# Moving eight modulation chunks, spreading transposes, and ordering a softmax behind a copy in an adaLN attention and FFN block

## The chip, the cores and the metric

The kernel runs on one core of a Trainium2 chip. The metric is the device time of one execution, in microseconds (us), lower being better. Times are medians of several executions, and all executions used here are fast. "Span" is the length of the one execution that was profiled; it was 1.7 to 2.2 us shorter than the time of the same execution in the runs here.

Names in the profile: PE is TensorE (matrix multiplications and transposes), PEld its weight loads, DVE is VectorE, ACT is ScalarE, POOL is GpSimd, and SP issues loads. PSUM is the memory that the matmuls here write to, and an eviction is a copy out of it. Each trace also keeps a record of the clock that TensorE was granted, the clock record below; a slow spell is a stretch of it at half clock. In the kernel before, one lasts from 63.33 to 66.74 us: matmuls with 512 columns start 0.43 us apart in it, and 0.215 us apart at full clock (from 55.63 us, for instance).

## The reference

```python
# x: (1, 2048, 1024), c: (1, 1024), w_mod: (1024, 6*1024), F = 3584
mod = (silu(c) @ w_mod).reshape(c.shape[0], 6, 1, -1)
sa, ca, ga, sb, cb, gb = mod[:, 0], ..., mod[:, 5]
h = layernorm(x) * (1 + ca) + sa
x = x + ga * A(h, wqkv, wo)          # 32 heads of 32; each position looks at 8 positions, 2 apart
h = layernorm(x) * (1 + cb) + sb
x = x + gb * B(h, w_gate, w_up, w_down)   # (sigmoid(h @ w_gate) * (h @ w_up)) @ w_down
```

## The kernel before

The 2048 rows are worked in four chunks of 512: chunks 0 and 1 are the first halves of the even and of the odd rows, chunks 2 and 3 the second halves. A chunk is projected to q, k and v on TensorE, which are stored to DRAM and loaded back in the layout that attention needs. Attention itself is VectorE's work: four units per chunk, each with products, sums, one Exp on ScalarE, and products again. Then TensorE transposes the attention result `Ot` into `oT`, multiplies it by `wo`, VectorE adds it to `X`, a second layernorm gives `Z`, TensorE transposes that into `h2T`, and the FFN follows.

The vector `mod` is made in twelve chunks of 512 columns. Each needs 1 MB of `w_mod`:

```python
    def mod_chunk(cc, col=None, add=0.0, dst=None, mul=1.0):
        wm = ring.tile([P, KT, 512], BF, name="wm", tag="w")
        nc.sync.dma_start(wm[:], w_mod[:, cc * 512:(cc + 1) * 512].rearrange(...))
        ps = ptile("aux", "ps_mod")
        for kt in range(KT):                       # 8 matmuls
            nc.tensor.matmul(ps[32 * j:32 * j + 32, :], sc_pad[:, kt, :], wm[:, kt, :], ...)
        part = small.tile([P, 512], BF, name="part")
        nc.scalar.copy(part[:], ps[:])             # ScalarE
        cv = ptile("aux", "cv")
        if dst is None:
            ...                                    # 4 small matmuls, then VectorE writes 4 columns
            nc.vector.tensor_scalar_add(modc[:, col:col + 4], cv[:, 0:4], add)
        else:
            ...
```

The order of the first half of the kernel is this. All eight later mod chunks stand between the layernorm of chunk 1 and the projection of chunk 0:

```python
    load_x(0)
    mod_cols(0, 0)                  # mod chunks 0 to 3
    ...                             # loads of wqkv and of X of chunk 1
    prep_chunk(0, tag="mm", split=True)   # layernorm, 32 transposes, evictions into hT
    for ci in range(NCH - 1):
        if ci + 2 < NCH:
            load_x(ci + 2)
        prep_chunk(ci + 1)
        if ci == 0:
            mod_bcast(4, ga_bc, 1.0)      # mod chunks 4, 5
            mod_cols(6, 2 * KT)           # 6 to 9
            mod_bcast(10, gbh_bc, 0.5)    # 10, 11
        ...                               # for the last: load wo and scale it by ga
        qkv_chunk(ci, range(NQ))
        if ci == 0:
            attention_chunk(0)            # at low priority: fills gaps on VectorE
    qkv_chunk(NCH - 1, range(NSPLIT))
    ...
    wo_chunk(0)
    qkv_chunk(NCH - 1, range(NSPLIT, NQ))
    ...
    for ci in range(NCH):
        if ci + 1 < NCH:
            attention_chunk(ci + 1)
            wo_chunk(ci + 1)
        ffn_a(ci)
        ffn_b(ci, last=(ci == NCH - 1))
```

A scheduler turns this into one fixed instruction order per engine before the kernel runs. In the trace of the kernel before, ScalarE keeps to its order even where it costs time: it stands idle for 6.23 us before an Exp while copies stand behind it whose transposes had ended at 192.35 us (below).

## Time and profile before

| | before |
|---|---|
| time, median (lowest to highest) | 900.81 us (899.01 to 902.83), 16 executions |
| span of the profile | 897.1 us |
| TensorE busy | 845.6 us |
| VectorE busy | 532.7 us, most of it before 504.6 us, where the last attention result is written |

From the profile's page of the kernel before: the busy time of each engine with its share of the span, and below it the rows in which each digit is one fortieth of the span (22.4 us) and gives the busy share in tenths.

```profile
PE 845.6 (94%) x4145; PEld 389.3 (43%) x4228; DVE 532.7 (59%) x652; ACT 194.8 (22%) x318; POOL 42.4 (5%) x71
...
PE   3979989969999999989999999999999999999997
...
DVE  4458999999799999999989612144121023121122
```

TensorE is nearly always busy, so its gaps are few and can be looked at one by one. VectorE is as full as TensorE in the first half of the kernel and has much room in the second.

The timeline of TensorE in the kernel before, at its three longest gaps between 30 and 245 us. The columns are start, duration, engine, line, operation, output and inputs, shapes, count; the bracket gives the idle time just before and what ended it.

```profile
63.62 1.04 PE L135 MATMUL ps_mod<-wm,sc_pad 128*32 128x512 bf16 x8 [4.37 <-DMA wm<-in_w_mod_dram]
...
129.28 0.61 PE L177 MATMUL tp<-ident,Xt 128*128 128x128 bf16 x8 [2.98 <-ACT hT L188]
...
199.67 1.01 PE L177 MATMUL tp<-ident,Ot 128*128 128x128 bf16 x8 [6.47 <-ACT oT L179]
```

The first is a wait for a mod chunk's weights. In the second, 32 transposes stand together, and each group of eight needs a PSUM buffer that ScalarE must have emptied. The third is a copy of transposes on ScalarE that came late. ScalarE's own timeline tells why:

```profile
191.49 0.59 ACT L237 CAST stg<-ps_qkv 128x512 bf16<-128x512 f32 x1 [1.14 <-PE ps_qkv L234]
198.31 0.42 ACT L282 ACTIVATE Et<-Lt 128x256 f32<-128x256 f32 x1 [6.23 <-DVE Lt L280]
198.63 1.91 ACT L179 COPY oT<-tp 128x1024 bf16<-128x1024 bf16 x2
```

ScalarE stood idle for 6.23 us for the Exp, whose input VectorE had not finished, and the copies that TensorE needed stood behind that Exp. The first two of those copies were ready to run: the sixteen transposes that they copy had ended at 192.35 us.

VectorE has its own waits. Its timeline in the kernel before, at the three longest after 50 us:

```profile
56.60 4.49 DVE L264 TENSOR_TENSOR prod<-qt,kh 128x4096 bf16<-128x4096 bf16 x2 [4.48 <-DMA qt<-qs]
...
70.03 0.16 DVE L143 TENSOR_SCALAR modc<-cv 128x4 f32<-128x4 f32 x1 [6.61 <-PE cv L142]
...
237.99 0.60 DVE L284 TENSOR_REDUCE sm<-Et 128x32 f32<-128x256 f32 x1 [4.75 <-ACT Et L282]
```

These are waits for the first q tile (loaded back from DRAM among the `w_mod` loads: its store took 9.0 us to land and its load 6.4), for a mod chunk on TensorE, and for an Exp.

### The profile page before, as it was taken

How to read it: one execution, taken by the hardware profiler on the slowest of the kernel's cores; microseconds unless marked ns; L12 is line 12 of the kernel's file. 1: busy time of each engine (PE TensorE's matmuls, PEld its weight loads, DVE VectorE, ACT ScalarE, POOL GpSimd, SP SyncE). 2: the span in 40 equal slices, each digit the busy share in tenths (PEclk: the TensorE clock that was granted, in tenths of full speed). 3: DMA queues.
4: the chain of work that ended last, by engine and by line, in shares of the span. 5: the costliest groups of instructions: out<-in, count | busy, mean ns of one | idle time of the engine just before them, and what ended most of it. 6: DMA issues, size and time to landing. Idle time of an engine off the chain costs nothing.

```text
span 897.1 us, 10091 instructions
## 1 busy us (share of the span) xinstructions
PE 845.6 (94%) x4145; PEld 389.3 (43%) x4228; DVE 532.7 (59%) x652; ACT 194.8 (22%) x318; POOL 42.4 (5%) x71
## 2 busy tenths in 40 slices
PE   3979989969999999989999999999999999999997
PEld 1434444434444444434444444444444444444443
DVE  4458999999799999999989612144121023121122
ACT  2436353331521232002132110023111001111100
POOL 0020100010100000001000000000000000000000
PEclk9999999989999999989999999999999999999999
DMA  9999847461345465757524455441544555453541
GB/s 304 359 335 373 287 167 266 151 236 40 114 164 171 126 213 184 269 172 254 181 94 140 142 164 164 157 172 47 188 129 141 165 175 173 156 179 108 175 149 47
DMA packets 125310, 162.20 MB, mean 181 GB/s; under 512 B 4160, under 2 KB 108608, under 8 KB 125264
## 3 DMA queue, kind: packets, MB, share of 16 engines
q1 hardware_dynamic: 117472, 126.95, 43.3%
q0 software_dynamic: 7792, 34.61, 11.1%
q8 instruction: 33, 0.54, 0.2%
q14 instruction: 13, 0.11, 0.0%
HBM read 144.71 MB, written 16.83 MB: 180 GB/s over the span
## 4 chain that ended last, share of the span: by engine, by line
PE 42%; DVE 32%; issue 18%; DMA 5%; ACT 2%; POOL 1%; SPq 0%; POOLq 0%; DVEq 0%; ACTq 0%
PE y L400 11%; PE ups L354 10%; PE gps L350 10%; DVE prod L264 6%; DVE prod L270 5%; DVE pv L292 5%; PE ps_qkv L234 4%; PE ps_wo L328 3%; DVE pv L297 3%; DVE hh L359 2%; DVE ln_st L161 2%; PE yl L389 2%; DMA wm<-in_w_mod_dram 2%; DVE pv L298 1%; PE tp L177 1%
## 5 line engine op out<-in xcount | busy, mean ns | idle before, releaser
L350 PE MATMUL gps<-h2T,wg 128*128 128x512 bf16 x874 | 212.8, 379 | 1.5 <-ACT stg L237 0.2
L354 PE MATMUL ups<-h2T,wu 128*128 128x512 bf16 x876 | 213.3, 379 | 0.9
L400 PE MATMUL y<-wd,hh 128*128 128x512 bf16 x770 | 172.1, 383 | 4.5 <-DVE ytmp L379 3.7
L359 DVE SCALAR_TENSOR_TENSOR hh<-th,ups 128x512 bf16<-128x512 f32 x112 | 76.5, 683 | 166.1 <-PE ups L354 157.4
L234 PE MATMUL ps_qkv<-wq,hT 128*128 128x512 bf16 x749 | 171.2, 382 | 1.3 <-issue 0.5
L357 ACT ACTIVATE th<-gps 128x512 f32<-128x512 f32 x112 | 66.9, 597 | 370.6 <-PE gps L350 303.7
L350 PEld LDWEIGHTS <-wg 128*128 128x128 bf16 x896 | 87.3, 98 | 103.1 <-issue 0.3
L354 PEld LDWEIGHTS <-wu 128*128 128x128 bf16 x896 | 87.3, 98 | 102.8
L400 PEld LDWEIGHTS <-hh 128*128 128x128 bf16 x784 | 77.3, 99 | 98.6 <-issue 7.6
L234 PEld LDWEIGHTS <-hT 128*128 128x128 bf16 x768 | 74.2, 98 | 89.2 <-issue 5.0
L379 DVE TENSOR_TENSOR ytmp<-y,gbh_bc 128x512 f32<-128x512 f32 x28 | 18.0, 682 | 107.9 <-PE y L400 107.9
L264 DVE TENSOR_TENSOR prod<-qt,kh 128x4096 bf16<-128x4096 bf16 x32 | 72.3, 2284 | 4.8 <-DMA qt<-qs 4.5
L270 DVE TENSOR_TENSOR prod<-prod 128x4096 bf16<-128x4096 bf16 (+1 forms) x64 | 73.7, 1152 | 1.3
L292 DVE TENSOR_TENSOR pv<-vh,A 128x4096 bf16<-128x4096 bf16 x32 | 72.3, 2286 | 0.4
L328 PE MATMUL ps_wo<-wo_sb,oT 128*128 128x512 bf16 x251 | 61.5, 382 | 1.5 <-DVE X L330 1.2
L239 ACT CAST stg<-ps_qkv 128x512 bf16<-128x512 f32 x64 | 37.0, 591 | 62.9 <-PE ps_qkv L234 61.8
L328 PEld LDWEIGHTS <-oT 128*128 128x128 bf16 x256 | 24.5, 99 | 32.9 <-issue 5.5
L297 DVE TENSOR_TENSOR pv<-pv 128x4096 bf16<-128x4096 bf16 x16 | 36.5, 2281 | 0.2
L179 ACT COPY oT<-tp 128x1024 bf16<-128x1024 bf16 x16 | 16.1, 1011 | 73.1 <-PE tp L177 73.0
L330 DVE TENSOR_TENSOR X<-ps_wo,X 128x512 bf16<-128x512 f32 x32 | 21.8, 684 | 11.0 <-PE ps_wo L328 6.4
L161 DVE BATCH_NORM_STATS2 ln_st<-Xt 128x6 f32<-128x512 bf16 x32 | 19.9, 665 | 12.3 <-DMA Xt<-in_A_x_dram 12.3
L188 ACT ACTIVATE h2T<-tp,modc 128x512 bf16<-128x512 bf16 x32 | 22.8, 778 | 10.8 <-PE tp L177 10.8
(64 smaller groups left out, 372.2 us busy)
## 6 DMA issues: line engine op xcount, KB each, us to landing
wg<-in_B_w_gate_dram SPq DMA_DIRECT2D x28, 1024.0 KB, 5.3
wu<-in_B_w_up_dram SPq DMA_DIRECT2D x28, 1024.0 KB, 7.2
wd<-in_B_w_down_dram SPq DMA_DIRECT2D x32, 896.0 KB, 5.2
wm<-in_w_mod_dram SPq DMA_DIRECT2D x12, 1024.0 KB, 8.1
kh<-ks POOLq DMA_DIRECT2D x16, 704.0 KB, 6.0
vh<-vs POOLq DMA_DIRECT2D x16, 704.0 KB, 4.7
wq<-in_A_wqkv_dram SPq DMA_DIRECT2D x6, 1024.0 KB, 12.5
Xt<-in_A_x_dram SPq DMA_DIRECT2D x4, 1024.0 KB, 9.4
```

What stands on the lines that cost most here:

```text
L161: nc.vector.bn_stats(st[:, b, hf, :], Xt[:, b, hf * 512:(hf + 1) * 512])
L234: nc.tensor.matmul(ps[:], hT[:, kt, b * P:(b + 1) * P], wt[:, kt, :], start=(kt == 0), stop=(kt == KT - 1))
L264: nc.vector.tensor_tensor(prod[:, 4 * i:4 * i + 4, :], qt[:].unsqueeze(1).to_broadcast([P, 4, QN]), win(kh, 4 * i, 4, QN), ALU.mult)
L270: nc.vector.tensor_tensor(pr[:, :, 0:n], pr[:, :, 0:n], pr[:, :, n:2 * n], ALU.add)
L292: nc.vector.tensor_tensor(pv[:, 4 * i:4 * i + 4, :].rearrange("p w (e u t) -> p w e u t", u=Dh // 2, t=2), win(vh, 4 * i, 4, QN).rearrange ...
L297: nc.vector.tensor_tensor(pv[:, 0:4, :], pv[:, 0:4, :], pv[:, 4:8, :], ALU.add)
L328: nc.tensor.matmul(ps[:], oT[:, kt, b * P:(b + 1) * P], wo_sb[:, kt, nh * 512:(nh + 1) * 512], start=(kt == 0), stop=(kt == KT - 1))
L350: nc.tensor.matmul(gps[:], wg[:, kt, fi * P:(fi + 1) * P], h2T[:, kt, :], start=(kt == 0), stop=(kt == KT - 1))
L354: nc.tensor.matmul(ups[:], wu[:, kt, fi * P:(fi + 1) * P], h2T[:, kt, :], start=(kt == 0), stop=(kt == KT - 1))
L357: nc.scalar.activation(th[:], gps[:], ACT.Tanh, scale=0.5)
L359: nc.vector.scalar_tensor_tensor(hh[:], th[:], 1.0, ups[:], ALU.add, ALU.mult)
L400: nc.tensor.matmul(ys[b][:], hhs[ft][:, b * P:(b + 1) * P], wd[:, fj, :], start=(ft == 0), stop=(ft == FT - 1))
```

## The change

The intent is to take away TensorE's three gaps. Four things are moved, and no arithmetic is dropped:

1. Eight of the twelve mod chunks go out of the crowded start into the projections of chunks 1 and 2, one every five groups. `mod_chunk` is cut in load, matmuls and columns.
2. The 32 transposes of a chunk's `X` are no longer one lump, but four steps of eight, each between two projection groups. The layernorm before them moves forward, for which `X` gets a third buffer.
3. At the start, the transposes of chunk 0 are put between mod chunks, in the order 0, 2, 1, 3.
4. Three Exps of attention chunk 1 get a rule that keeps them behind the `oT` copies of chunk 0 on ScalarE.

The diff, cut to its core:

```diff
-    xz_pool = phA_left.enter_context(tc.tile_pool(name="xz", bufs=2))
+    xz_pool = phA_left.enter_context(tc.tile_pool(name="xz", bufs=3))
@@ ...                                    (mod_chunk becomes mod_load, mod_mm, mod_cv)
@@ def qkv_chunk
             for b in range(J):
+                for f in (hooks or {}).get(i * J + b, ()):
+                    f()
                 ps = ptile("mm", "ps_qkv")
@@ def attention_unit
-        nc.scalar.activation(Et[:], Lt[:], ACT.Exp, scale=SCALE)
+        ex = nc.scalar.activation(Et[:], Lt[:], ACT.Exp, scale=SCALE)
+        if ci == 1 and hg in (1, 2, 3):
+            tc.add_manual_dep(ex.ins, oT_last[0].ins.name, mybir.DependencyInfo(
+                mybir.DependencyClass.NoSync, mybir.DependencyReason.DATA), reason="Exp after the oT copies")
@@ the start
-    mod_cols(0, 0)
+    wms = {cc: mod_load(cc) for cc in (0, 2, 1, 3)}
@@ ...                                    (loads of wqkv as before)
+    ln1_chunk(0)
+    t0t, t0e = t1_steps(0, tag="mm", split=True, separate=True)
+    for n, cc in enumerate((0, 2, 1, 3)):
+        part = mod_mm(wms.pop(cc), "aux")
+        mod_cv(part, "aux", col=MODCOL[cc][0], add=MODCOL[cc][1])
+        if n == 0:
+            for f in t0t:
+                f()
+        elif n == 1:
+            t0e[0](), t0e[1]()
+        elif n == 3:
+            t0e[2](), t0e[3]()
@@ the loop over chunks
     for ci in range(NCH - 1):
+        hooks = {g: [] for g in range(NGRP)}
         if ci + 2 < NCH:
-            load_x(ci + 2)
-        prep_chunk(ci + 1)
-        if ci == 0:
-            mod_bcast(4, ga_bc, 1.0)
-            mod_cols(6, 2 * KT)
-            mod_bcast(10, gbh_bc, 0.5)
+            hooks[0].append(lambda ci=ci: load_x(ci + 2))
+        hooks[2].append(lambda ci=ci: ln1_chunk(ci + 1))
+        steps = []
+        hooks[12].append(lambda ci=ci: steps.extend(t1_steps(ci + 1)))
+        for n in range(4):
+            hooks[12 + 2 * n].append(lambda n=n: steps[n]())
         if ci + 1 == NCH - 1:
@@ ...                                    (load of wo becomes a hook at group 20)
+        if ci in (1, 2):
+            for n in range(4):
+                k = (ci - 1) * 4 + n
+                hooks[1 + 5 * n].append(lambda k=k: mod_a(k))
+                hooks[2 + 5 * n].append(lambda k=k: mod_b(k))
-        qkv_chunk(ci, range(NQ))
+        qkv_chunk(ci, range(NQ), hooks)
```

More of the change, by code (lines that the diff above doesn't have):

```diff
@@ L60 @@
     USE_DMAT = False
+    last_copy = [None]
     LOW = 10_000_000
@@ L127, with mod_load, mod_mm @@
     gbh_bc = const.tile([P, D], BF, name="gbh_bc")
-    def mod_chunk(cc, col=None, add=0.0, dst=None, mul=1.0):
+    def mod_load(cc):
         wm = ring.tile([P, KT, 512], BF, name="wm", tag="w")
         nc.sync.dma_start(wm[:], w_mod[:, cc * 512:(cc + 1) * 512].rearrange("(k p) n -> p k n", p=P))
-        ps = ptile("aux", "ps_mod")
+        return wm
+    def mod_mm(wm, tag):
+        ps = ptile(tag, "ps_mod")
         for kt in range(KT):
@@ L138, in mod_chunk, with mod_cv @@
         nc.scalar.copy(part[:], ps[:])
-        cv = ptile("aux", "cv")
+        return part
+    def mod_cv(part, tag, col=None, add=0.0, dst=None, mul=1.0):
+        cv = ptile(tag, "cv")
         if dst is None:
@@ L146, in mod_chunk @@
             nc.scalar.mul(dst, cv[:], mul)
-    def mod_cols(cc0, col0):
-        for i in range(4):
-            mod_chunk(cc0 + i, col=col0 + 4 * i, add=(0.0 if i < 2 else 1.0))
-    def mod_bcast(cc0, dst, mul):
-        for i in range(2):
-            mod_chunk(cc0 + i, dst=dst[:, i * 512:(i + 1) * 512], mul=mul)
     def layernorm(Xt, Zt):
@@ L169, in layernorm, with transpose_steps, step_t @@
                                     ALU.subtract, ALU.mult)
-    def transpose_chunk(Zt, dstT, col0=None, tag="tp", split=False):
-        for k2 in range(KT // 2):
+    def transpose_steps(Zt, dstT, col0=None, tag="tp", split=False, separate=False):
+        tps = {}
+        def step_t(k2):
             tp = ptile(tag, "tp", [P, 2, NPOS], BF)
+            tps[k2] = tp
             for kk in range(2):
@@ L177, in transpose_chunk, with step_e @@
                     nc.tensor.transpose(tp[:, kk, b * P:(b + 1) * P], Zt[:, b, kt * P:(kt + 1) * P], ident[:])
+        def step_e(k2):
+            tp = tps.pop(k2)
             if col0 is None:
-                nc.scalar.copy(dstT[:, 2 * k2:2 * k2 + 2, :], tp[:])
+                last_copy[0] = nc.scalar.copy(dstT[:, 2 * k2:2 * k2 + 2, :], tp[:])
             else:
@@ L190, in transpose_chunk @@
                                              scale=modc[:, col0 + KT + kt:col0 + KT + kt + 1])
+        ts = [(lambda k2=k2: step_t(k2)) for k2 in range(KT // 2)]
+        es = [(lambda k2=k2: step_e(k2)) for k2 in range(KT // 2)]
+        if separate:
+            return ts, es
+        return [(lambda k2=k2: (ts[k2](), es[k2]())) for k2 in range(KT // 2)]
+    def transpose_chunk(*a, **kw):
+        for f in transpose_steps(*a, **kw):
+            f()
     def transpose_chunk_dma(Zt, dstT, col0=None):
@@ L210 @@
     Xts, hTs = {}, {}
+    oT_last = [None]
     def load_x(ci):
@@ L215, in load_x, with ln1_chunk, t1_steps, qkv_chunk @@
         Xts[ci] = Xt
-    def prep_chunk(ci, **kw):
-        Xt = Xts.pop(ci)
+    def ln1_chunk(ci):
+        Xt = Xts[ci]
         layernorm(Xt, Xt)
+    def t1_steps(ci, **kw):
         hT = hT_pool.tile([P, KT, NPOS], BF, name="hT")
-        transpose_chunk(Xt, hT, col0=0, **kw)
         hTs[ci] = hT
-    def qkv_chunk(ci, idxs):
+        return transpose_steps(Xts.pop(ci), hT, col0=0, **kw)
+    def qkv_chunk(ci, idxs, hooks=None):
         r, t0 = chunks[ci]
@@ L321, in wo_chunk @@
         oT = pb["oT"].tile([P, KT, NPOS], BF, name="oT")
-        (transpose_chunk_dma if (USE_DMAT and ci > 0) else transpose_chunk)(Ot, oT)
+        transpose_chunk(Ot, oT)
+        oT_last[0] = last_copy[0]
         wo_sb = pb["wo_sb"]
@@ L412 @@
         load_wqkv(i)
+    ln1_chunk(0)
+    t0t, t0e = t1_steps(0, tag="mm", split=True, separate=True)
+    MODCOL = {0: (0, 0.0), 1: (4, 0.0), 2: (KT, 1.0), 3: (KT + 4, 1.0)}
+    for n, cc in enumerate((0, 2, 1, 3)):
[3 more added lines that the diff above has]
+            for f in t0t:
+                f()
+        elif n == 1:
+            t0e[0](), t0e[1]()
+        elif n == 3:
+            t0e[2](), t0e[3]()
     zt = ring.tile([P, KT, 512], BF, name="zt", tag="w")
@@ L417 @@
     nc.sync.dma_start(vs[:, :, 0:HALO, :].rearrange("r g t d -> (r g) (t d)"), ztv)
-    prep_chunk(0, tag="mm", split=True)
     ga_t = ring.tile([P, KT, 512], BF, name="ga_t", tag="w")
     ga_bc = ga_t[:, 0:2, :].rearrange("p a b -> p (a b)")
+    MODREST = [(4, dict(dst=ga_bc[:, 0:512])), (5, dict(dst=ga_bc[:, 512:1024])),
+               (6, dict(col=2 * KT)), (7, dict(col=2 * KT + 4)),
+               (8, dict(col=3 * KT, add=1.0)), (9, dict(col=3 * KT + 4, add=1.0)),
+               (10, dict(dst=gbh_bc[:, 0:512], mul=0.5)), (11, dict(dst=gbh_bc[:, 512:1024], mul=0.5))]
@@ new lines, with mod_a, mod_b, load_wo @@
+    mod_state = {}
+    def mod_a(k):
+        mod_state[k] = mod_mm(mod_load(MODREST[k][0]), "mm")
+    def mod_b(k):
+        mod_cv(mod_state.pop(k), "mm", **MODREST[k][1])
+    def load_wo():
+        phA_left.close()
+        wo_pool = ctx.enter_context(tc.tile_pool(name="wo", bufs=1))
+        wo_sb = wo_pool.tile([P, KT, D], BF, name="wo_sb")
+        nc.sync.dma_start(wo_sb[:], A_wo.rearrange("(k p) n -> p k n", p=P))
+        nc.vector.tensor_tensor(wo_sb[:], wo_sb[:], ga_bc.unsqueeze(1).to_broadcast([P, KT, D]), ALU.mult)
+        pb["wo_sb"] = wo_sb
@@ L422 @@
+    NGRP = NQ * J
     for ci in range(NCH - 1):
+        hooks = {g: [] for g in range(NGRP)}
         if ci + 2 < NCH:
-            load_x(ci + 2)
-        prep_chunk(ci + 1)
-        if ci == 0:
-            mod_bcast(4, ga_bc, 1.0)
-            mod_cols(6, 2 * KT)
-            mod_bcast(10, gbh_bc, 0.5)
-        if ci + 1 == NCH - 1:
-            phA_left.close()
-            wo_pool = ctx.enter_context(tc.tile_pool(name="wo", bufs=1))
-            wo_sb = wo_pool.tile([P, KT, D], BF, name="wo_sb")
-            nc.sync.dma_start(wo_sb[:], A_wo.rearrange("(k p) n -> p k n", p=P))
-            nc.vector.tensor_tensor(wo_sb[:], wo_sb[:], ga_bc.unsqueeze(1).to_broadcast([P, KT, D]), ALU.mult)
-            pb["wo_sb"] = wo_sb
@@ L437 @@
-        qkv_chunk(ci, range(NQ))
+            hooks[0].append(lambda ci=ci: load_x(ci + 2))
[4 more added lines that the diff above has]
+            hooks[12 + 2 * n].append(lambda n=n: steps[n]())
+        if ci + 1 == NCH - 1:
+            hooks[20].append(load_wo)
+        if ci in (1, 2):
[3 more added lines that the diff above has]
+                hooks[2 + 5 * n].append(lambda k=k: mod_b(k))
```

## The prediction

> **What bounds it now.** TensorE: the page's busy table gives PE 845.6 of 897.1 us, VectorE 532.7, full until about 460 us. PE's timeline shows its idle stretches. From 245 us on they are about 1 us each (3.7 once). Before it:
> - startup: the first projection matmul starts at 22.9 us, after four mod chunks (9.98 us wait for the first w_mod load);
> - 4.37 us before 63.6 us: PE waits in order for a w_mod load. The DMA share is 0.98 to 1.09 from 23 to 88 us;
> - 2.98 us before 129 us: 32 transposes in a lump wait for ScalarE's hT evictions (eight at a stretch);
> - 6.47 us before 199.7 us: transposes wait for the oT copy, which stands in ScalarE's queue behind an Exp that waits 6.23 us for VectorE.
>
> After the first and last of these waits the granted clock falls (0.93 and 0.77 in those stretches): matmuls start 0.43 us apart instead of 0.215. [...] I estimate 1.5 + 1.1 us of slow matmuls.
>
> **What the change does.** No arithmetic goes away (8458 PE instructions in both orders). It moves eight mod chunks into chunks 1 and 2, taking 8 MB from the saturated DMA stretch; spreads the transposes between projection groups; pulls layernorms forward with a third X buffer; keeps three Exps behind the oT copies. [...]
>
> Sum, in us:
> - w_mod wait gone: -4.4, cold clock -1.5
> - transpose lump gone: -3.0; small waits beside the mod chunks: -0.6
> - oT wait gone: -6.5, cold clock -1.1
> - startup: +1.3. In the new order the second mod chunk finishes after the transposes, and the third chunk's copy stands behind two hT evictions on ScalarE, so the last mod chunk ends about 1 us later.
> - wo chunk 0: VectorE's first X addition now comes after the sum and reciprocal of an attention unit, and 38 wo matmuls run in a row on two PSUM buffers: +1.8. Its Z transposes wait longer: +1.0.
>
> Net about -13. It stays only if VectorE comes forward too: attention chunk 1 gates PE at 274.6 us with almost no slack. VectorE's first attention product should start at about 50 instead of 56.6 us (q, k stores no longer behind w_mod), and its 6.6 us wait for mod columns at 63 to 70 us goes: also about 13. All of it is on the critical path; what follows 275 us just shifts.
>
> **Prediction:** 889 us, 882.5 to 896. Faster by over 2% 0.10, within 2% 0.88, slower 0.02.
>
> **What would show it.** Right: FFN gate matmuls start near 227 us (240.2 now); no PE wait on w_mod after startup; the oT and hT waits gone; granted clock near 1.00 from 30 to 245 us; first attention product near 50 us; the rest as long as before within 3 us. Wrong: first projection matmul before 22.9 us; PE waits over 5 us for X or Z at the wo chunk; a PE wait of several us for Ot of chunk 1.
>
> **What would make it wrong.** Exps that block ScalarE longer than four projection buffers can hide (about 5 us) in chunks 1 and 2; q, k, v stores queued behind w_mod loads that wait for ring buffers; or VectorE getting ahead, so that its later waits (3.7 us at 389 us) vanish and the gain passes 2%.

The trace of the kernel before shows this. The clock record has half clock from 63.33 to 66.74 us and from 196.45 to 203.28 us; the means 0.93 and 0.77 are those of 60 to 85 and of 190 to 205 us. That these spells would go with the waits was the author's estimate. The 1.5 us is half of the 3.12 us that TensorE is busy in the first; the 1.1 us is taken up below. The DMA share from 23 to 88 us is 1.04 in the mean, with 0.87 from 45 to 56 us. That four projection buffers hide about 5 us is an estimate too (three groups of eight matmuls, 0.215 us apart, take 5.2 us).

## The result, and the profile after

| | before | after |
|---|---|---|
| time, median (lowest to highest) | 900.81 us (899.01 to 902.83), 16 executions | 888.52 us (887.22 to 890.36), 7 executions |
| span of the profile | 897.1 us | 886.1 us |
| TensorE busy | 845.6 us | 843.9 us |
| TensorE idle in gaps of 0.15 us or more, added up from its timeline | 42.2 us | 32.7 us |
| first projection matmul | 22.94 us | 24.08 us |
| first attention product on VectorE | 56.60 us | 51.73 us |
| first FFN gate matmul | 240.24 us | 228.72 us |
| transposes of the last unit of attention chunk 1 | 274.57 us | 263.02 us |

The ratio of after to before is 0.9867, with a 95% interval of 0.9854 to 0.988. A ratio here is the mean time of one kernel's fast executions over the mean of the kernel before's in the same rounds, so it is not quite the ratio of the medians. The kernel is 1.3% faster: within 2%, and close to the predicted 889 us. All outputs are right.

The page of the kernel after, the same rows as above:

```profile
PE 843.9 (95%) x4146; PEld 387.2 (44%) x4228; DVE 532.9 (60%) x652; ACT 194.5 (22%) x318; POOL 42.3 (5%) x71
...
PE   3999999989999999899999999999999999999997
...
DVE  4488999999999999998989412244121023212122
```

In the old row of TensorE the third digit is 7 and the ninth is 6: those slices hold the gaps of 4.37 and 6.47 us. Both digits are higher now. Both engines do the same work as before in less time.

TensorE's timeline after. The longest gap between 30 and 245 us is now this one:

```profile
193.56 5.34 PE L351 MATMUL ps_wo<-wo_sb,oT 128*128 128x512 bf16 x24 [2.22 <-DVE X L353]
```

None of the three old gaps is left. In their place is one wait of 2.22 us (the next longest, 1.77 us, is for the columns of a moved mod chunk): the products with `wo` fill their two PSUM buffers until VectorE makes its first addition to `X`. ScalarE's timeline after shows the effect of the rule:

```profile
185.62 3.77 ACT L184 COPY oT<-tp 128x1024 bf16<-128x1024 bf16 x4
...
191.54 0.42 ACT L301 ACTIVATE Et<-Lt 128x256 f32<-128x256 f32 x1 [2.16 <-DVE Lt L299]
```

The four copies now come first, and ScalarE waits for VectorE's Exp input only afterwards, when nobody needs ScalarE.

VectorE's timeline after, at the places that answer to the ones shown of before (the wait for a mod column is gone altogether):

```profile
51.73 2.29 DVE L283 TENSOR_TENSOR prod<-qt,kh 128x4096 bf16<-128x4096 bf16 x1 [2.73 <-DMA qt<-qs]
...
226.40 0.60 DVE L306 TENSOR_REDUCE sm<-Et 128x32 f32<-128x256 f32 x1 [0.54 <-ACT Et L301]
```

The medians differ by 12.3 us and these two profiled executions by 11.0 us of span, because the profiled execution of the kernel before (899.23 us) was 1.6 us faster than its median and that of the kernel after 0.4 us. The account below is of the profiled ones. Where did the 11.0 us of the span come from? In both kernels VectorE begins the layernorm of chunk 2 when its `X` lands, at 43.48 and 43.50 us. That is a common starting point. From there to the end of the last attention unit of the kernel, VectorE does the same work in both. The view of one stretch gives, for each engine, busy time and count, then granted clock, DMA share and GB/s; first the kernel before, then the kernel after:

```profile
43.40:504.57 461.17, 434.25 (x2178) 199.94 (x2220) 425.00 (x457) 132.74 (x220) 36.07 (x57) 0.98 0.58 195
```

```profile
43.40:493.62 450.22, 432.81 (x2203) 199.88 (x2245) 425.17 (x457) 134.82 (x223) 35.97 (x57) 0.99 0.59 200
```

The busy numbers stand in the order PE, PEld, DVE, ACT, POOL. VectorE is busy for 425.00 and 425.17 us with 457 instructions in both. Its idle time is what is left of the stretch: 461.17 - 425.00 = 36.2 us before and 450.22 - 425.17 = 25.1 us after. The difference, 11.1 us, is the whole gain but for a tenth of a us, and what follows the stretch takes 392.5 us in both kernels. This is bookkeeping and not yet a proof that VectorE sets the pace: any engine that does the same work in a stretch must account for its change. TensorE's gaps over the whole kernel shrink by 9.5 us and its busy time by 1.7 us, the latter partly because slow matmuls count as busy for longer (between 63 and 67 us of the kernel before the `qkv` matmuls are recorded with 379 ns at the least and 620 ns in the median). Which engine sets the pace is what e6, e7 and e8 test.

VectorE's waits in the part of this stretch up to the end of attention chunk 1 (273.8 us before, 262.3 us after), where the kernels part by 11.6 us. The columns are what waited, what for, us in total, times, longest. Before:

```profile
DVE sm L284 <- ACT Et L282: 7.8, 7, 4.8
DVE modc L143 <- PE cv L142: 6.8, 2, 6.6
DVE prod L264 <- DMA qt<-qs: 4.5, 1, 4.5
...
DVE Xt L168 <- POOL ln_rstd L166: 2.2, 2, 1.2
```

After:

```profile
...
DVE Xt L167 <- POOL ln_rstd L165: 3.7, 2, 2.5
DVE sm L306 <- ACT Et L301: 3.5, 7, 0.5
DVE prod L283 <- DMA qt<-qs: 2.7, 1, 2.7
```

The wait for mod columns is gone (-6.8), the waits for Exp shrank (-4.3), the wait for the first q tile shrank (-1.8), and the wait for `ln_rstd` grew (+1.5): together -11.4 us of the 11.6.

### The profile page after: what moved, and what is told of

The parts are those of the page before. It is cut to its first block, busy times and chain, and to the rows that moved or that the text cites. A ratio compares the mean times of both kernels' runs of the same rounds, so it can differ in the third digit from the quotient of the medians.

```text
span 886.1 us, 10085 instructions
## 1 busy us (share of the span) xinstructions
PE 843.9 (95%) x4146; PEld 387.2 (44%) x4228; DVE 532.9 (60%) x652; ACT 194.5 (22%) x318; POOL 42.3 (5%) x71
## 4 chain that ended last, share of the span: by engine, by line
PE 45%; DVE 31%; issue 18%; DMA 4%; ACT 1%; POOL 1%; SPq 0%; POOLq 0%; DVEq 0%; ACTq 0%
PE gps L373 12%; PE ups L377 12%; PE y L423 11%; PE ps_qkv L253 5%; DVE pv L314 5%; DVE prod L283 5%; DVE prod L289 5%; DVE pv L319 3%; PE yl L412 2%; DVE ln_st L160 2%; DVE hh L382 2%; DVE X L353 2%; PE ps_wo L351 2%; DVE pv L320 1%; PE tp L179 1%
## 5 line engine op out<-in xcount | busy, mean ns | idle before, releaser
L160 DVE BATCH_NORM_STATS2 ln_st<-Xt 128x6 f32<-128x512 bf16 x32 | 19.9, 665 | 11.1 <-DMA Xt<-in_A_x_dram 11.1
```

## The experiments

Two theories went into the runs.

- P: TensorE sets the time. Its waits are separate terms, and each one that goes away pays for itself.
- V: VectorE's attention chain sets the time of the first part of the kernel. TensorE's waits in that part are mostly slack; taking one away only lets TensorE wait elsewhere. V put the end of that part at about 265 us.

### e1: the rule alone

The kernel before, with nothing but the rule that three Exps stay behind the `oT` copies.

```diff
-        nc.scalar.activation(Et[:], Lt[:], ACT.Exp, scale=SCALE)
+        ex = nc.scalar.activation(Et[:], Lt[:], ACT.Exp, scale=SCALE)
+        if ci == 1 and hg in (1, 2, 3):
+            tc.add_manual_dep(ex.ins, oT_last[0].ins.name, ...)
```

> The kernel before with only the rule that three Exps come behind the oT copies. Theory P (the gain is a sum of TensorE waits, each pays by itself): the 6.5 us oT wait and 1.1 us of slow clock go, about 2 us come back at the wo chunk: 895 to 896 us, ratio 0.994. Theory V (up to about 265 us VectorE's attention chain sets the pace, and what TensorE saves before it is spent again waiting for VectorE): VectorE's first attention product stays at 56.6 us, so 899 to 901 us, ratio 0.998 to 1.001; TensorE's waits for Ot of chunk 1 and for X and Z at the wo chunk grow from 2.6 us to 7 us or more.

Measured: 896.18 us, ratio 0.9961 (0.9944 to 0.9977), 4.1 us less than the kernel before in the same rounds (900.25 us). The number is that of P. But the first attention product did not come earlier (57.05 us), and the last unit of attention chunk 1 was still written 4.15 us earlier (269.67 for 273.82 us). VectorE had gained after all: the Exp that it had waited 4.75 us for came after 0.54 us. So the rule also helped VectorE, which neither theory nor the prediction had said. The run does not decide between the two.

### e2: everything but the rule

```diff
-        if ci == 1 and hg in (1, 2, 3):
+        if False:
             tc.add_manual_dep(ex.ins, ...)
```

> The changed kernel without that rule. In its instruction order one Exp stands ahead of the four oT copies again. Theory P: plus 7.6 us, minus 2.8 us because the waits for X and Z at the wo chunk go: 893 us. Theory V: VectorE loses nothing, and TensorE has only the 5 us that it now waits for X, Z and Ot to absorb the loss with: 889 to 891 us, and those waits shrink by what the oT wait costs.

Measured: 895.68 us, ratio 0.995 (0.9937 to 0.9963). Without the rule the changed kernel loses 7.2 us, more than both theories said. TensorE's timeline of this run shows the old gap again:

```profile
194.21 1.01 PE L179 MATMUL tp<-ident,Ot 128*128 128x128 bf16 x8 [6.76 <-ACT oT L184]
```

VectorE waits for Exps 11.7 us in all up to its last attention result, for 8.1 us with the rule.

### e3: the mod chunks alone

The kernel before, with only the eight later mod chunks moved into the projections of chunks 1 and 2. Transposes, start and Exps are those of before.

```diff
-        if ci == 0:
-            mod_bcast(4, ga_bc, 1.0)
-            mod_cols(6, 2 * KT)
-            mod_bcast(10, gbh_bc, 0.5)
+        hooks = {}
+        if ci in (1, 2):
+            for n in range(4):
+                k = (ci - 1) * 4 + n
+                hooks.setdefault(1 + 5 * n, []).append(lambda k=k: mod_a(k))
+                hooks.setdefault(2 + 5 * n, []).append(lambda k=k: mod_b(k))
```

> The kernel before with only the eight later mod chunks moved into chunks 1 and 2. Theory P: the w_mod wait, its slow clock and the small waits go, 6.5 us: 894 us, ratio 0.993, and the oT wait stays at about 6.5 us. Theory V: VectorE's first product comes at about 51 us instead of 56.6 and its 6.6 us wait for mod columns goes, so almost the whole gain is here: 889 to 891 us, ratio 0.987 to 0.989, and the oT wait shrinks without any rule, because the Exp waits for VectorE.

Measured: 887.93 us, ratio 0.987 (0.9853 to 0.9886). One of the four parts has the whole gain, so the parts do not add: by the medians of their own rounds e1 gained 4.1, e3 12.3, and all together 12.3 us. The ratio is V's (the time is 1 us under its range), but the way is not: VectorE wrote its last attention result only at 500.63 us, 7 us later than in the changed kernel. The reason is that the scheduler gave other places to work that the edit does not name: two transposes and copies of `oT` went ahead to 122 us, so that the 6.47 us gap was gone without the rule, and more FFN matmuls went ahead of VectorE's late results (TensorE had 441.67 us of busy time behind it at that point, for 432.81 in the changed kernel). A wait of another kind came:

```profile
194.10 6.26 PE L340 MATMUL ps_wo<-wo_sb,oT 128*128 128x512 bf16 x17 [4.09 <-DVE X L342]
```

Seventeen recorded matmuls take 6.26 us there, about 0.37 us each, where full speed is about 0.22; the 4.09 us gap was followed by half-speed matmuls. The run shows that moving the chunks is enough for the gain. It is not a clean measure of that part, because the order changed elsewhere.

### e4: the transposes in one lump again

```diff
         for n in range(4):
-            hooks[12 + 2 * n].append(lambda n=n: steps[n]())
+            hooks[12].append(lambda n=n: steps[n]())
```

> The changed kernel with the four transpose steps of a chunk in one lump at group 12 instead of two groups apart. Theory P: the 3 us wait for the hT evictions comes back, in each of three chunks where it is not hidden: plus 3 us or more, 891.5 us. Theory V: TensorE waits for ScalarE at the lumps, but later waits for VectorE shrink by as much: within 1 us of the changed kernel.

Measured: 892.26 us, ratio 0.991 (0.9892 to 0.9928), 3.7 us more than the changed kernel. P had this number. Here too the scheduler changed more than the lump: 62 matmuls with `wo` stand in a row, the wait for `X` there is 3.32 us, and VectorE's last result comes at 502.22 us. So the number can't be put down to the lump alone.

### e5 and e6: the start

e5 is the changed kernel with the start of before. e6 is the changed kernel with the transposes of chunk 0 one mod chunk later, which takes the wait at the start away. In both the order of the instructions differs from the changed kernel only in the start.

```diff
# e5
-    wms = {cc: mod_load(cc) for cc in (0, 2, 1, 3)}
+    for cc, col, add in ((0, 0, 0.0), (1, 4, 0.0), (2, KT, 1.0), (3, KT + 4, 1.0)):
+        mod_cv(mod_mm(mod_load(cc), "aux"), "aux", col=col, add=add)
@@ ...                    (ln1_chunk(0) and all transposes of chunk 0 come after it)
# e6
-        if n == 0:
+        if n == 1:
             for f in t0t:
                 f()
-        elif n == 1:
             t0e[0](), t0e[1]()
```

> The changed kernel with the startup of the kernel before (mod chunks in their old order, transposes of chunk 0 after all of them); all else in the instruction order is the same. If the startup term of the prediction (plus 1.3 us) is right: the first projection matmul starts at 22.9 us instead of 24.1, and the time falls by about 1.1 us, to 887.4. If VectorE's chain sets the pace, the first product does not come earlier than 51 us and the time stays within 0.3 us.

> The changed kernel with the chunk-0 transposes issued after the second mod chunk instead of after the first: the only difference is the order of ten pieces on TensorE, so that the second mod chunk ends about 3 us earlier and its hT evictions are out of ScalarE's way. The first projection matmul should start at 21.9 to 22.3 us (its weights land at about 21.9) instead of 24.1. If each us of startup counts: 886.4 us, minus 2 us. If VectorE sets the pace: within 0.5 us.

Measured: e5 888.86 us, ratio 0.9867 (0.9851 to 0.9883); e6 887.83 us, ratio 0.986 (0.9845 to 0.9875). The first projection matmul starts at 22.52 and 21.83 us, for 24.08 in the changed kernel, and neither kernel is faster by more than the noise. In e5 this tests little: its slow spell at the start lasts 6.8 us for 3.4 in the changed kernel (24.87 to 28.28 us), and by its next transposes (46.14 for 46.70 us) TensorE is only 0.56 us ahead. In e6 TensorE is there at 42.82 us, 3.9 us ahead, and loses this lead as V says. ScalarE's timeline of the changed kernel, then of e6, then TensorE's of e6:

```profile
97.88 0.42 ACT L301 ACTIVATE Et<-Lt 128x256 f32<-128x256 f32 x1 [2.46 <-DVE Lt L299]
```

```profile
97.18 0.42 ACT L301 ACTIVATE Et<-Lt 128x256 f32<-128x256 f32 x1 [5.06 <-DVE Lt L299]
```

```profile
102.27 0.25 PE L149 MATMUL cv<-selcol,part 128*128 128x1 bf16 x4 [2.26 <-ACT part L142]
```

ScalarE waits for VectorE's Exp input as before, only longer, and a copy that TensorE needs stands behind it. This wait and the slow spell after it (3.4 us at half clock, by estimate half of it lost, about 1.7 us) leave TensorE 0.7 us ahead at the next mod chunk (121.03 for 121.70 us). VectorE's last attention result comes at 493.49 and 493.20 us, for 493.62. In the stretch of e6 VectorE's idle time is 449.80 - 425.07 = 24.7 us, practically that of the changed kernel (25.1):

```profile
43.40:493.20 449.80, 433.36 (x2223) 198.39 (x2221) 425.07 (x457) 133.16 (x221) 36.72 (x57) 0.99 0.60 200
```

Its waits only changed names: `ln_rstd` fell from 3.7 to 0.9 us and the q tile rose from 2.7 to 4.9 us.

### e7 and e8: more work on one engine

These two put a known amount of work on one engine, with the same results. e7 repeats 24 projection matmuls (about 24 x 0.215 = 5.2 us of TensorE) in the projection of chunk 1. e8 repeats two attention products (4.5 us of VectorE) in the second unit of chunk 0, and leaves TensorE's order as it is.

```diff
# e7
-                for kt in range(KT):
-                    nc.tensor.matmul(ps[:], hT[:, kt, b * P:(b + 1) * P], wt[:, kt, :], ...)
+                for rep in range(2 if (ci == 1 and i == 3 and b < 3) else 1):
+                    for kt in range(KT):
+                        nc.tensor.matmul(ps[:], hT[:, kt, b * P:(b + 1) * P], wt[:, kt, :], ...)
# e8
-        for i in range(2):
+        for i in [0, 1] * (2 if (ci == 0 and hg == 1) else 1):
             nc.vector.tensor_tensor(prod[:, 4 * i:4 * i + 4, :], ...)
```

> The changed kernel with 24 projection matmuls of chunk 1 done twice, 5.2 us more work for TensorE at about 95 us, results unchanged. If TensorE is the limit there: plus 4.5 to 5.2 us. If VectorE is: the waits of TensorE for X, Z and Ot up to 263 us (5.3 us in all in the changed kernel) shrink by most of it and the time grows by 0 to 2 us.

> The changed kernel with the two first products of one attention unit of chunk 0 done twice, 4.5 us more work for VectorE at about 90 us, results unchanged; TensorE's order is the same. If VectorE is the limit up to 263 us: plus 4 to 4.5 us, as longer waits for X or Ot. If TensorE is and VectorE has room: plus 0 to 1.5 us. If the two are balanced, both this and the run with more matmuls cost 3 us or more.

Measured: e7 891.15 us, ratio 0.9905 (0.9879 to 0.9931), span 888.2 us; e8 893.85 us, ratio 0.9927 (0.9912 to 0.9942), span 890.8 us. What the added work cost depends on the measure: 2.1 us in e7 and 4.7 in e8 by the two spans, 2.6 and 5.3 by the medians, 3.4 and 5.4 by the ratios, of which that of e7 has a wide interval. The attention results show where it went. The first one of chunk 0 starts at 85.85 us in the changed kernel, 87.09 in e7 and 86.48 in e8, still without the added work; the last of chunk 1 starts at 262.27, 266.56 and 268.89 us. So 3.0 of TensorE's 5.2 us arrive at that point, and 6.0 us for VectorE's 4.5 (TensorE's wait for `X` grew from 2.22 to 4.99 us in e8, and a slow spell of 6.8 us followed). Where the work was put, TensorE had about 2 us of room and VectorE had none. That is near the third case, two engines almost in balance. After 398 us both kernels regain 1.9 us. There VectorE waits for TensorE in the changed kernel (1.09 us at 402.32 us) and not in these two, whose slow spell near 380 us is 3.4 us long instead of 6.8; that this is the reason is not shown. The stretches of e7 and e8:

```profile
43.40:496.02 452.62, 440.69 (x2277) 202.73 (x2276) 424.96 (x457) 135.26 (x224) 35.98 (x57) 1.00 0.60 199
```

```profile
43.40:498.36 454.96, 437.24 (x2247) 200.80 (x2246) 429.62 (x459) 135.65 (x223) 35.99 (x57) 0.98 0.59 198
```

In e8 VectorE is busy 4.45 us longer and idle 25.3 us, as in the changed kernel. In e7 it is idle for 27.7 us, 2.6 more: the added matmuls made ScalarE's Exps and the normalisations later (the waits for Exp rise from 8.1 to 11.2 us, those for `ln_rstd` from 3.7 to 5.3). The longest of them is the Exp at 195.76 us, which the new rule keeps behind the `oT` copies (192.15 us here, 185.62 in the changed kernel): VectorE waits 3.39 us for it. So the rule has a price where TensorE is late.

### e9: a shorter wait at the end of the down projection

With the start settled, the largest wait left on TensorE after the first projection is 3.57 us at 377.48 us, where four PSUM tiles of the down projection finish together and VectorE has to empty one. The clock record has a slow spell of 6.8 us from 376.44 us on. e9 finishes the four tiles one after another in the last quarter.

```diff
-                for fj in range(FPB):
-                    ft = wb * FPB + fj
-                    for b in range(J):
+                order = [(fj, b) for fj in range(FPB) for b in range(J)]
+                if wb == NWB - 1:
+                    order = [(fj, b) for b in range(J) for fj in range(FPB)]
+                for fj, b in order:
+                        ft = wb * FPB + fj
```

> The changed kernel with another order of the last quarter of the down projection: tile by tile instead of all four output tiles in turn, so that the first output tile is finished 21 matmuls (4.5 us) before the last and VectorE can empty it in time. TensorE's 3.6 us wait for VectorE at 377 us should go, and with it the 6.8 us of half clock after it (3.4 us): 881.5 to 883 us. If VectorE's backlog there is the limit whatever TensorE does, the wait moves to a later place and the time stays at 887 or more.

Measured: 893.06 us, ratio 0.9911 (0.9895 to 0.9928): a clear miss, 4.5 us slower than the changed kernel instead of 5 to 7 faster. The wait fell to 1.19 us and the slow spell went away. VectorE's last result came 1.1 us earlier. But TensorE now arrived early at two additions to `X`, and waited there. TensorE's timeline of the changed kernel at the wait that was to go, then that of e9:

```profile
377.48 3.14 PE L423 MATMUL y<-wd,hh 128*128 128x512 bf16 x7 [3.57 <-DVE ytmp L402]
```

```profile
420.29 3.21 PE L351 MATMUL ps_wo<-wo_sb,oT 128*128 128x512 bf16 x8 [4.26 <-DVE X L353]
...
586.38 3.15 PE L351 MATMUL ps_wo<-wo_sb,oT 128*128 128x512 bf16 x8 [3.23 <-DVE X L353]
```

The first was 0.84 us before this edit. VectorE is busy almost without a gap up to that addition, which stands at a fixed place of its order. At the second it is VectorE that waits:

```profile
585.63 0.69 DVE L353 TENSOR_TENSOR X<-ps_wo,X 128x512 bf16<-128x512 f32 x1 [3.20 <-DMA X<-in_A_x_dram]
```

The changed kernel has this wait for the load of `X` too (3.08 us), but there TensorE lost only 0.30 us to it. Eight matmuls take 3.15 us at 586.38 us instead of the usual 1.89, at half speed. What follows VectorE's last attention result took 399.0 us for 392.5. The longer wait (2.9 us), the slow spell (half of 3.4 us) and ten more matmuls behind that point (1832 weight loads for 1822, about 2.2 us) add up to 6.8 us for these 6.5.

### e10 and e11: earlier loads

e10 loads `X` of chunk 2 before the last two parts of `wqkv`, because VectorE waits 4.33 us for that `X` at 43.50 us. e11 is e10, e6 and e9 together.

```diff
# e10
-    for i in range(3, NQ):
-        load_wqkv(i)
+    load_wqkv(3)
@@ ...                    (in qkv_chunk, wq_sb[i] is read inside the inner loop)
@@ the loop over chunks
+    load_x(2)
     for ci in range(NCH - 1):
         hooks = {g: [] for g in range(NGRP)}
-        if ci + 2 < NCH:
+        if ci == 0:
+            hooks[4].append(lambda: load_wqkv(4))
+            hooks[8].append(lambda: load_wqkv(5))
+        elif ci + 2 < NCH:
```

> The changed kernel with only the loads in another order: X of chunk 2 before the last two projection weights, which come behind the first k and q stores. If VectorE's chain, which starts when X of chunk 2 lands (43.5 us in both kernels), sets the pace up to 263 us: X lands at about 37 us, the first product starts at about 46 us instead of 51.7, the last Ot of chunk 1 comes 3 to 5 us earlier and the time falls by 2.5 to 4.5 us, to 884 to 886 (TensorE had about 3 us of room in the run with more matmuls). If the sum of TensorE's own waits is what counts, nothing changes: 888 to 889 us.

> The changed kernel with the new load order, the early start and the tile-by-tile end of the down projection together. If VectorE limits up to 263 us and TensorE has 3 us plus the 2.2 us of the early start as room: 887.5 minus 4.5 to 5.5 minus 6 us, 876 to 878 us. If the early start stays worthless: 879 to 880 us.

Measured: e10 890.35 us, ratio 0.9873 (0.9844 to 0.9901); e11 894.36 us, ratio 0.9926 (0.9907 to 0.9945). Both miss. `X` landed earlier (4.3 us of VectorE's work lies before 43.40 us), but the wait for it only made room for a longer one: VectorE's first product stood at 57.24 us in e10, after 9.17 us of waiting for the first q tile, and an Exp wait of 4.03 us came back, for the same Exp behind the `oT` copies as in e7. In e11 the waits of e9 came on top (5.14 us at 421.54 and 2.89 us at 587.43).

### e12: one more buffer for X

In the trace of e9 loads of `X` in the second half wait for the write of an earlier chunk's result (8.6 us, two times), because they share buffers. e12 is the changed kernel with e6, e9 and one more buffer, for the `X` of chunk 2.

```diff
-        X1 = pb["x1"].tile([P, J, D], BF, name="X1")
+        X1 = pb["x1b" if ci == 2 else "x1"].tile([P, J, D], BF, name="X1")
@@ ...
+    pb["x1b"] = ctx.enter_context(tc.tile_pool(name="x1b", bufs=1, side="right"))
```

> The changed kernel with the early start, the tile-by-tile end of the down projection and a third buffer for X in the second half (for chunk 2 alone), so that X of chunk 2 need not wait until the output of chunk 0 is written. In the run with the tile-by-tile end alone TensorE's wait moved from 377 us to 420 and 586 us, to X additions whose X load waits for an output write. If that write is the cause, those two waits (4.3 and 3.2 us there) fall under 1 us, no half clock follows, and the time is 880 to 882 us, clear of the changed kernel. If VectorE's backlog holds TensorE at 420 us whatever the buffer, the wait stays and the time is 888 us or more.

Measured: 886.49 us, ratio 0.9849 (0.9833 to 0.9866). It is the fastest median of all, but its interval overlaps with that of the changed kernel (0.9854 to 0.988), so it is not shown to be faster, and 880 to 882 was missed. Two of TensorE's waits are gone (the 3.57 us is 1.21, the one at 586 us is gone), and one is longer. TensorE's timeline, and VectorE's at the same time:

```profile
411.24 3.17 PE L351 MATMUL ps_wo<-wo_sb,oT 128*128 128x512 bf16 x8 [3.50 <-DVE X L353]
```

```profile
403.17 2.28 DVE L283 TENSOR_TENSOR prod<-qt,kh 128x4096 bf16<-128x4096 bf16 x1
405.37 0.68 DVE L403 TENSOR_TENSOR X<-ytmp,X 128x512 bf16<-128x512 f32 x1
405.97 2.29 DVE L283 TENSOR_TENSOR prod<-qt,kh 128x4096 bf16<-128x4096 bf16 x1
408.29 2.29 DVE L289 TENSOR_TENSOR prod<-prod 128x4096 bf16<-128x4096 bf16 x1
410.50 0.68 DVE L353 TENSOR_TENSOR X<-ps_wo,X 128x512 bf16<-128x512 f32 x1
```

The addition to `X` that TensorE waits for (410.50) follows without a gap on attention work. The buffer was not the limit any more: VectorE was simply busy. Its idle time in the stretch is 449.86 - 424.70 = 25.2 us, as in the changed kernel.

### All runs in one table

The stretch runs from 43.40 us to the end of VectorE's last attention result. "Idle" is its length less VectorE's busy time in it; "rest" is the span less the end of the stretch. All in us.

| kernel | time | span | VectorE's last result | VectorE idle | rest |
|---|---|---|---|---|---|
| before | 900.81 | 897.1 | 504.57 | 36.2 | 392.5 |
| after | 888.52 | 886.1 | 493.62 | 25.1 | 392.5 |
| e1, rule alone | 896.18 | 893.2 | 500.41 | 32.0 | 392.8 |
| e2, no rule | 895.68 | 892.1 | 497.20 | 29.5 | 394.9 |
| e3, mod chunks alone | 887.93 | 888.4 | 500.63 | 31.4 | 387.8 |
| e4, lump | 892.26 | 893.0 | 502.22 | 34.0 | 390.8 |
| e5, old start | 888.86 | 886.3 | 493.49 | 24.9 | 392.8 |
| e6, earlier start | 887.83 | 885.7 | 493.20 | 24.7 | 392.5 |
| e7, TensorE +5.2 | 891.15 | 888.2 | 496.02 | 27.7 | 392.2 |
| e8, VectorE +4.5 | 893.85 | 890.8 | 498.36 | 25.3 (busy 4.45 longer) | 392.4 |
| e9, down projection | 893.06 | 891.5 | 492.50 | 24.9 | 399.0 |
| e10, loads | 890.35 | 890.4 | 497.93 | 33.6 (4.3 of its work lies ahead of the stretch) | 392.5 |
| e11, e10 + e6 + e9 | 894.36 | 892.6 | 493.89 | 29.1 (3.8 lies ahead) | 398.7 |
| e12, third buffer | 886.49 | 885.3 | 493.26 | 25.2 | 392.0 |

The profiled executions of e3, e4 and e10 were some 2 us longer than these kernels' median, which is why their spans stand high against their times.

In nine of the fourteen kernels the rest is 392.0 to 392.8 us, and the span follows VectorE's last result. In e2, e3 and e4 the rest differs by 1.7 to 4.7 us because more or less of TensorE's work lies behind that point. The weight loads there count it: 1822 in the kernels before and after (1821 or 1822 in all nine), 1833 in e2, 1801 in e3, 1815 in e4, 1832 in e9 and 1831 in e11. At 0.215 us each these differences are +2.4, -4.5, -1.5, +2.2 and +1.9 us; in e9 and e11 longer waits (2.9 and 2.6 us) and a slow spell (about 1.7 us) come on top. That explains every rest to 0.3 us. So the account has a condition: it holds for kernels with the same order of TensorE's late work. The end of the stretch was chosen after the runs; the theory had it at 265 us, its numbers for e1, e2, e4 and e9 to e12 were wrong, and those for e7 and e8 too low. The delays of e7 and e8 at the end of chunk 1 do not depend on that choice.

## Why the prediction was right or wrong

The number was right: 889 us predicted, 888.52 measured, within 2%. So were most of its steps.

- "w_mod wait gone", "transpose lump gone", "oT wait gone": right. All three gaps are missing from TensorE's timeline after, and e2 brings the third back at 6.76 us by undoing the rule alone.
- "wo chunk 0: +1.8": right. A wait of 2.22 us for the first addition to `X` came up. "Z transposes wait longer: +1.0" was too much; the longest such wait there went from 0.93 to 1.28 us.
- "FFN gate matmuls start near 227 us": 228.72. "First attention product near 50 us": 51.73. "Granted clock near 1.00 from 30 to 245 us": 1.00, after 0.98 before. "The rest as long as before within 3 us": after attention chunk 1 (274.57 and 263.02 us) 622.5 and 623.1 us remain.
- "It stays only if VectorE comes forward too ... also about 13": this was the decisive sentence, and it held: 11.6 us to the end of chunk 1 and 11.0 us to the last attention result. Its terms did not (below).

The terms that were off:

- "Startup: +1.3" was a real shift (22.94 to 24.08 us) and no cost. e6 moves that start by 2.25 us, and the time stays within noise.
- "oT wait gone: -6.5, cold clock -1.1": the second number was too small. The clock record has half clock from 196.45 to 203.28 us, and TensorE was busy for 3.39 us of it. Half of that, about 1.7 us, is the better estimate.
- "First attention product at about 50 instead of 56.6": it came 4.87 us earlier, but this was not 4.87 us gained. Between 43.4 us and the first product VectorE was busy for 7.36 us before and 5.44 us after; a normalisation of 1.9 us had only moved behind the product. The waiting shrank by 2.95 us. A start time is not a gain when the order of the work changes as well.
- One gain on VectorE was not named at all: the Exp behind a run of eight `h2T` evictions on ScalarE, 4.75 us before and 0.54 us after. The mod-column wait (-6.8) was named and measured as predicted. The forecast for VectorE came near by luck: of the 6.6 us named for the first product only about 3 us were less waiting, the wait for `ln_rstd` grew again by 1.5 us up to the end of chunk 1, and the unnamed 4.3 us filled the hole.
- "TensorE" as the bound was half of the truth. In the first half VectorE has no room and TensorE about 2 us (e8 against e7), and a lead of 3.9 us on TensorE is lost to VectorE by way of ScalarE (e6). That TensorE's sum gave nearly the same number is luck in part: the change took away about as much waiting on one engine as on the other. Had the sum alone been the reason, e6 would have been faster by about 2 us, and e9 and e12 by 5 to 8 us as was expected of them. e6 and e12 are not faster clear of noise, and e9 is slower.

What stays open: how much of the gain belongs to each of the four parts. The parts do not add, and in e3 and e4 the scheduler changed orders that the edits did not touch. Whether the mod chunks alone (887.93 us) are as good as the whole change is not separated by the intervals either; it looks so, by another order. Between 398 and 494 us both engines wait for each other, and which of them limits there was not tested.

## What to carry to other kernels

When two engines are both nearly full, choose a point from which both kernels do the same work, and list what each engine waits for up to a later common point. Either list can add up to the gain, so it doesn't tell which engine to predict with; adding a known amount of work to each engine in turn, and following the delay to the common point, does. Busy shares did not tell it here: from 43.40 to 493.62 us of the kernel after TensorE is the fuller of the two, 432.81 us against VectorE's 425.17, and still 5.2 us more on it cost 3.0 us up to the end of chunk 1 (e7), while 4.5 us more on VectorE cost 6.0 (e8).

In e9 a wait that was taken from TensorE moved to the next place where it meets VectorE: 3.57 us became 1.19 at one place, and 0.84 became 4.26 at the next. After new waits of 2.26 us (e6), 4.09 us (e3) and 4.99 us (e8) a slow spell followed: in e6 eight projection matmuls took 3.33 us instead of 1.89. The length of a gap alone did not tell whether one follows: after the same gap of 2.98 us, for ScalarE's `hT` evictions, the next eight transposes took 1.01 us in e1 and 0.61 us in the kernel before, and after the 2.22 us at 193.56 us of the kernel after the clock stayed at 1.00. What decides it was not shown.

ScalarE, with its copies and Exps in one order, couples the other two in these kernels. In the kernel before, an Exp ahead of the `oT` copies left ScalarE idle for 6.23 us and TensorE for 6.47 us, and eight evictions ahead of another Exp let VectorE wait 4.75 us. So look for an instruction that is put too early in the order of such an engine.
